# Loading the first tile of x in two column parts, and transposing the second tile among the first products

## The chip, the cores and the metric

The kernel runs on one core of one Trainium2 chip. The metric is the device time of one execution in microseconds (us). Three executions of the kernel before took 219.65, 219.71 and 219.72 us, median 219.71.

## What is computed

x is 2048 x 640, bf16. It is normalised by rows (LayerNorm without weights); on the result run a linear attention of 32 heads of 20 columns and a ReLU feed-forward of width 1728, and the two are joined:

```python
x = A_x
xn = _layernorm(x, axis=-1)
s = _A_ref(xn, A_wqkv, A_wo)              # q,k,v = xn @ wqkv; phi(q), phi(k); o = num / den; o @ wo
g = _silu(_B_ref(xn, B_w1, B_w2))         # relu(xn @ w1) @ w2
return x + s * g
```

What matters here is the beginning of the second branch, h = relu(xn @ w1), for the first 512 rows of x. A row's scale (one over its standard deviation) is positive and can be applied after the ReLU, so for these rows the kernel multiplies w1 with x minus its row mean, and applies the scale later (`rsy`).

## The kernel before

x is cut into 16 tiles of 128 rows (`t`), its 640 columns into 5 chunks of 128 (`C`). TensorE needs x transposed: `xnT` holds it as 5 chunks of 128 columns by 2048 rows. h is computed transposed, in 13 blocks `f` of 128 columns of w1 (and a half one) by 512 rows of x (`j`). All matmuls of one block add up over the 5 chunks in one of the 8 banks of PSUM (`ps[b]`).

The order of the work is written out by hand. `Sched` only collects, for each engine, its operations in the order of the calls, and derives the waits from the keys that each operation reads (`R`) and writes (`W`); each engine then runs its own list strictly in order. There are two queues that issue DMAs: SyncE's (SP), on which nearly all are issued, and ScalarE's (ACT).

The start, in the lines that the change touches:

- Loads (lines 370 to 375): x0 on SP, x1 on ACT, x2 on SP, the first piece of w1 (384 columns, blocks 0 to 2) on ACT, the second piece (256 columns, blocks 3 and 4) and x3 on SP. `x_load` is line 337, `w1_load` and `w_load` lines 364 and 341.
- `fill` (line 356) issues matmuls of constants, whose result nobody reads. Line 614 asks for nine.
- `T_mean` (line 422): the row mean of one tile, as a pass that scales by 1/640 and accumulates; on VectorE for tile 0 (line 428), on ScalarE for the others (line 424). `center` (line 434) subtracts the mean from some chunks, on VectorE (line 435). `T_pe` (line 439) transposes chunks on TensorE into a bank (line 441). `T_copy` (line 444) brings them from the bank to `xnT`, on ScalarE (line 448) or VectorE (line 451).
- `H_mm` (line 574) multiplies chunks `ks` of one block of w1 with columns of `xnT`; its matmuls are line 575. `H_first(t, fs, ks)` (line 608) does that for the 128 rows of tile t and the blocks fs; after tile 3 the block goes through ReLU on ScalarE (line 582).

The calls of lines 614 to 656 give the order: fillers; mean, centring, transposes and copies of tile 0, with those of tile 1 right behind; then the products of tile 0 with blocks 0 to 2; then tile 1's products, tile 2's transposes, and so on, with the later blocks and tiles behind. `w_load` of the key weights (line 628) waits for the second centring of tile 0, `w1_load(2)` (line 634) for the centring of tile 2, and the loads of x4 to x7, the last piece of w1 and the query weights are queued on SP behind them. `LN_stats` and `LN_norm` (lines 394 and 411) compute the exact mean and variance of a tile on VectorE later, and read the same tiles of x.

Of the kernel before, what the change touches and what calls it, by code (L numbers as in the profile page):

```python
# [210 lines left out]
def bass_recurrent_scan__linear_attn_block__dense_activation_relu__prompt_kernel(  # L211
# [14 lines left out]
    P = 128  # L226
# [75 lines left out]
    mhalf = nc.alloc_sbuf_tensor("mhalf", [P, 1], f32)  # L302
    denS = nc.alloc_sbuf_tensor("denS", [P, 512], f32)
    rden = nc.alloc_sbuf_tensor("rden", [P, 512], bf)
    mean = nc.alloc_sbuf_tensor("mean", [P, 4], f32)
    stats = nc.alloc_sbuf_tensor("stats", [P, T, 2, 6], f32)
    mv = nc.alloc_sbuf_tensor("mv", [P, T, 2], f32)
    rsv = nc.alloc_sbuf_tensor("rsv", [P, T], f32)
# [22 lines left out]
    def tok(t):  # L331
        return slice(P * t, P * (t + 1))
# [4 lines left out]
    def x_load(t, extra=(), E="SP"):  # L337
        sl = t % XR
        return dma(E, lambda eng: eng.dma_start(xin[:, sl, :], x2[tok(t), :]), W=[("xin", sl)], extra=extra)
# [16 lines left out]
    def fill(n, w=512):  # L356
        sc.group("PE", [(lambda eng: eng.matmul(ps[0][:, 0:w], lhsT=cones, rhs=cwide[:, 0:w], start=True, stop=True))
                        for _ in range(n)], W=[("ps", 0)])
# [5 lines left out]
    def w1_load(i, extra=(), E="SP"):  # L364
        w_load(w1_sb[:, :, W1C[i]:W1C[i + 1]], B_w1[:, W1C[i]:W1C[i + 1]], ("w1", i), extra, E)
# [1 line left out]
    def w1_part(f):  # L367
        return [i for i in range(NP) if W1C[i] <= P * f < W1C[i + 1]][0]

    x_load(0)  # L370
    x_load(1, E="ACT")
    x_load(2)
    w1_load(0, E="ACT")
    w1_load(1)
    x_load(3)

# [17 lines left out]
    def LN_stats(t):  # L394
        xv = xin[:, t % XR, :]
        for a in range(2):
            sc.op("DVE", lambda eng, a=a: eng.bn_stats(stats[:, t, a, :], xv[:, HN * a:HN * (a + 1)]),  # L397
                  R=[("xin", t % XR)], W=[("stats", t, a)])
        sc.op("DVE", lambda eng: eng.bn_aggr(mv[:, t, :], stats[:, t, :, :].rearrange("p a b -> p (a b)")),
              R=[("stats", t, 0), ("stats", t, 1)], W=[("mv", t)])  # L400
        sc.op("POOL", lambda eng: eng.tensor_scalar(out=rsv[:, t:t + 1], in0=mv[:, t, 1:2], scalar1=EPS_LN,
                                                    scalar2=None, op0=ALU.add), R=[("mv", t)], W=[("rsv", t)])
        sc.op("POOL", lambda eng: eng.tensor_tensor(out=rsy[:, t:t + 1], in0=rsv[:, t:t + 1], in1=mhalf[:, :],
                                                    op=ALU.pow), R=[("rsv", t), ("mhalf",)], W=[("rsy", t)])
# [3 lines left out]
    def xnk(t, cs=range(C)):  # L408
        return [("xn", t, c) for c in cs]

    def LN_norm(t, turn=False):
        last_norm[0] = sc.op("DVE", lambda eng: eng.tensor_scalar(
            out=xn[:, t, :], in0=xin[:, t % XR, :], scalar1=mv[:, t, 0:1], scalar2=rsy[:, t:t + 1],
            op0=ALU.subtract, op1=ALU.mult), R=[("xin", t % XR), ("mv", t), ("rsy", t)], W=xnk(t))
        if turn:
            xnT_dma(t)
        elif t + XR < T:
            x_load(t + XR)

    def T_mean(t, E="ACT"):
        if E == "ACT":
            sc.op("ACT", lambda eng: eng.activation(out=ek[:, 0, 0, :], in_=xin[:, t, :], func=ACTF.Copy, scale=1.0 / D,
                                                    accum_out=mean[:, t:t + 1]),
                  R=[("xin", t)], W=[("mean", t), ("ek_e", 0)])
        else:
            sc.op("DVE", lambda eng: eng.tensor_scalar(out=ek[:, 1, 0, :], in0=xin[:, t, :], scalar1=1.0 / D, scalar2=0.0,
                                                       op0=ALU.mult, op1=ALU.add, accum_out=mean[:, t:t + 1]),
                  R=[("xin", t)], W=[("mean", t), ("ek_e", 1)])  # L430

    sc.allow_unread.update([("ek_e", 0), ("ek_e", 1)])

    def center(t, c0, c1):
        return sc.op("DVE", lambda eng: eng.tensor_scalar(
            out=xn[:, t, P * c0:P * c1], in0=xin[:, t, P * c0:P * c1], scalar1=mean[:, t:t + 1], scalar2=None,
            op0=ALU.subtract), R=[("xin", t), ("mean", t)], W=xnk(t, range(c0, c1)))

    def T_pe(t, c0, c1, b):
        psb = ps[b].bitcast(bf)  # L440
# [3 lines left out]
    def T_copy(E, t, c0, c1, b):  # L444
        out = xnT[:, c0:c1, tok(t)]
        src = ps[b].bitcast(bf)[:, P * c0:P * c1].rearrange("p (c q) -> p c q", c=c1 - c0)
        if E == "ACT":
            sc.op("ACT", lambda eng: eng.activation(out=out, in_=src, func=ACTF.Copy), R=[("ps", b)],
                  W=xtk(t, range(c0, c1)))
        else:  # L450
            sc.op("DVE", lambda eng: eng.tensor_copy(out, src), R=[("ps", b)], W=xtk(t, range(c0, c1)))
# [159 lines left out]
            if t == 3:  # L611
                H_ev(0, f, HF[f])

    fill(9)
    T_mean(0, "DVE")
    T_mean(1)
    center(0, 0, 2)
    T_pe(0, 0, 2, 7)
    held = center(0, 2, 5)
    T_pe(0, 2, 5, 1)  # L620
    T_copy("ACT", 0, 0, 2, 7)
    center(1, 0, C)
    T_copy("DVE", 0, 2, 5, 1)
    T_pe(1, 0, 2, 0)
    T_pe(1, 2, 5, HF[4])
    T_copy("ACT", 1, 0, 2, 0)
    T_copy("DVE", 1, 2, 5, HF[4])
    w_load(wqk[:, :, D:2 * D], A_wqkv[:, D:2 * D], ("wk",), [held])
    H_first(0, (0, 1, 2), (0, 1))
    H_first(0, (0, 1, 2), (2, 3, 4))  # L630
    T_mean(2)
    held = center(2, 0, C)
    H_first(1, (0, 1, 2))
    w1_load(2, [held])
    x_load(4)
    x_load(5)
# [467 lines left out]
```

## Time and profile before

| what | value |
|---|---|
| median of three executions | 219.71 us |
| the profiled execution, its own time | 219.73 us |
| its span | 217.9 us |
| ScalarE's first pass over tile 2 (line 424) | starts at 6.18 us |
| ScalarE's copy of tile 3 (line 448) | starts at 9.76 us |
| key products (line 466) | start at 12.07 us |

The span runs from the first to the last instruction that the profiler recorded. In rows of the timeline the first number is the start and the second the duration in us; then come the engine, the line of the kernel, the operation, what it writes and reads, and in brackets how long the engine had been idle and what ended that. Here "psT" is PSUM, "reg" stands for several buffers (x, w1, xn, xnT), "SPq" and "ACTq" are the queues on which SyncE and ScalarE issue DMAs. PE is TensorE, PEld its weight loads, DVE VectorE, ACT ScalarE, POOL GpSimd.

### The profile page before, as it was taken

Reading aid. Unit: us, or ns where it says so; the run is one execution under the profiler, and the core shown is the slowest. Engines: PE = TensorE matmul, PEld = TensorE weight load, DVE = VectorE, ACT = ScalarE, POOL = GpSimd, SP = SyncE. Lnnn points to the kernel's source line nnn. Section 1 sums busy time; section 2 is a strip of 40 time slices with the busy share of each in tenths; the row PEclk is TensorE's granted clock in tenths of the full one; section 3 lists DMA queues with packets and bytes.
Section 4 is the critical chain, followed back from the end, with each engine's and each line's share of the span. In section 5 each row is a group of like instructions: output and inputs, shape, how many; then the busy total and the mean of one; then the engine's idle time right before and its main releaser. Section 6 shows DMA issues by size and latency. Waiting matters only on the chain.

```text
span 217.9 us, 3064 instructions
## 1 busy us (share of the span) xinstructions
PE 213.2 (98%) x1195; PEld 109.2 (50%) x1215; DVE 106.5 (49%) x196; ACT 92.8 (43%) x179; POOL 28.5 (13%) x59
## 2 busy tenths in 40 slices
PE   8999999999999999999999999999999999999995
PEld 2975444444444444444464446544444446555574
DVE  2788899994894757666700005711121122230354
ACT  3577558666775669955321213514110211101220
POOL 1155022041110000100000000000000003960001
DMA  6998668612236423660069988769312113334152
GB/s 204 292 386 130 150 178 206 138 24 51 54 79 120 84 51 78 120 140 0 3 194 365 232 146 256 288 188 352 52 24 44 31 24 65 69 115 148 24 168 91
DMA packets 48491, 29.24 MB, mean 134 GB/s; under 512 B 31492, under 2 KB 47836, under 8 KB 48476
## 3 DMA queue, kind: packets, MB, share of 16 engines
q1 hardware_dynamic: 47532, 28.29, 49.6%
q10 hardware_dynamic: 944, 0.75, 1.0%
q8 instruction: 9, 0.15, 0.3%
q14 instruction: 6, 0.05, 0.1%
HBM read 15.75 MB, written 5.24 MB: 96 GB/s over the span
## 4 chain that ended last, share of the span: by engine, by line
PE 96%; DMA 1%; DVE 1%; issue 1%
PE psT L575 26%; PE psT L879 19%; PE psT L560 10%; PE psT L829 8%; PE psT L503 7%; PE psT L922 7%; PE psT L886 7%; PE psT L957 3%; PE psT L466 2%; PE psT L818 2%; DMA reg<-in_A_x_dram 1%; PE psT L597 1%; PE psT L901 1%; PE psT L838 1%; PE psT L849 1%; PE psT L441 1%
## 5 line engine op out<-in xcount | busy, mean ns | idle before, releaser
L575 PE MATMUL psT<-reg 128*128 128x512 bf16 (+1 forms) x328 | 60.5, 330 | 0.5 <-issue 0.2
L879 PE MATMUL psT<-hT,reg 128*128 128x512 bf16 x191 | 44.2, 379 | 0.3
L575 PEld LDWEIGHTS psT<-reg 128*128 128x128 bf16 x335 | 28.6, 98 | 27.5 <-issue 0.4
L582 ACT ACTIVATE hT<-psT 128x512 bf16<-128x512 f32 x52 | 30.6, 598 | 16.0 <-PE psT L575 15.9
L929 DVE TENSOR_TENSOR er<-psT,ek 128x512 bf16<-128x512 f32 x15 | 10.4, 692 | 48.4 <-PE psT L922 45.2
L879 PEld LDWEIGHTS psT<-hT,reg 128*128 128x128 bf16 x195 | 18.9, 98 | 22.3 <-issue 0.7
L917 ACT ACTIVATE ek<-psT 128x512 bf16<-128x512 f32 x15 | 8.3, 599 | 42.3 <-PE psT L904 21.9
L560 PE MATMUL psT<-reg 128*128 128x512 bf16 x100 | 24.8, 379 | 0.0
L937 POOL TENSOR_TENSOR reg<-reg 128x640 bf16<-128x640 bf16 x8 | 10.9, 1392 | 90.9 <-DMA reg<-er 90.9
L568 DVE TENSOR_SCALAR er<-psT 128x512 bf16<-128x512 f32 x20 | 13.7, 686 | 8.9 <-ACT er L567 8.9
L503 PE MATMUL psT<-reg 128*128 128x512 bf16 x72 | 17.8, 379 | 0.2
L922 PE MATMUL psT<-pqT,reg 128*128 128x512 bf16 x71 | 17.3, 379 | 0.2
L829 PE MATMUL psT<-reg 128*128 128x512 bf16 x78 | 17.3, 379 | 0.1
L560 PEld LDWEIGHTS psT<-reg 128*128 128x128 bf16 x100 | 9.8, 98 | 11.8
L886 PE MATMUL psT<-reg,hT 128*128 128x320 bf16 x104 | 15.3, 299 | 0.0
L512 DVE TENSOR_SCALAR ek<-psT 128x512 bf16<-128x512 f32 x15 | 10.1, 676 | 9.3 <-ACT ek L511 9.3
L567 ACT ACTIVATE er<-psT 128x512 bf16<-128x512 f32 x20 | 12.0, 598 | 5.5 <-PE psT L560 5.5
L397 DVE BATCH_NORM_STATS2 stats<-reg 128x6 f32<-128x320 bf16 x32 | 13.8, 474 | 0.7 <-DMA reg<-in_A_x_dram 0.6
L570 DVE SCALAR_TENSOR_TENSOR pqT<-er 128x512 bf16<-128x512 bf16 x20 | 13.8, 692 | 0.7
L841 DVE TENSOR_TENSOR reg<-psT,m 120x120 bf16<-120x120 f32 x6 | 1.7, 282 | 23.4 <-PE psT L838 23.4
L886 PEld LDWEIGHTS psT<-reg,hT 128*128 128x128 bf16 x104 | 10.1, 98 | 4.8 <-issue 0.3
L829 PEld LDWEIGHTS psT<-reg 128*128 128x128 bf16 x80 | 7.8, 98 | 9.3
(77 smaller groups left out, 183.4 us busy)
## 6 DMA issues: line engine op xcount, KB each, us to landing
rscr<-rden SPq DMA_DIRECT2D x4, 640.0 KB, 8.2
reg<-rscr SPq DMA_DIRECT2D x5, 512.0 KB, 6.8
reg<-in_A_x_dram SPq DMA_DIRECT2D x4, 640.0 KB, 6.1
reg<-in_A_x_dram SPq DMA_DIRECT2D x15, 160.0 KB, 3.2
out_dram<-reg SPq DMA_DIRECT2D x15, 160.0 KB, 1.9
reg<-in_A_wqkv_dram SPq DMA_DIRECT2D x2, 800.0 KB, 4.7
reg<-in_B_w_dram SPq DMA_DIRECT2D x1, 1120.0 KB
reg<-in_B_w_dram SPq DMA_DIRECT2D x1, 960.0 KB, 8.0
```

What stands on the lines that cost most here:

```text
L397: sc.op("DVE", lambda eng, a=a: eng.bn_stats(stats[:, t, a, :], xv[:, HN * a:HN * (a + 1)]), R=[("xin", t % XR)], W=[("stats", t, a)])
L503: lastK[0] = sc.group("PE", [(lambda eng, k=k: eng.matmul(ps[b], lhsT=wqk[:, k, D + P * m:D + P * (m + 1)], rhs=xnT[:, k, schunk(j)], star ...
L560: sc.group("PE", [(lambda eng, k=k: eng.matmul(ps[b], lhsT=wqk[:, k, P * f:P * (f + 1)], rhs=rhs(k), start=(k == 0), stop=(k == C - 1))) f ...
L567: sc.op("ACT", lambda eng: eng.activation(out=e_, in_=ps[b], func=ACTF.Exp), R=[("ps", b)], W=[("er_e", es)])
L568: sc.op("DVE", lambda eng: eng.tensor_scalar(out=r_, in0=ps[b], scalar1=0.0, scalar2=1e-6, op0=ALU.max, op1=ALU.add), R=[("ps", b), ("er_e ...
L570: sc.op("DVE", lambda eng: eng.scalar_tensor_tensor(out=pqT[:, f, schunk(j)], in0=e_, scalar=1.0, in1=r_, op0=ALU.min, op1=ALU.add), R=[(" ...
L575: return sc.group("PE", [(lambda eng, k=k: eng.matmul(ps[b][:, lo:hi], lhsT=w1_sb[:, k, P * f:P * (f + 1)], rhs=xnT[:, k, 512 * j + lo:512 ...
L582: sc.op("ACT", lambda eng: eng.activation(out=hT[:, f, schunk(j)], in_=ps[b], func=ACTF.Relu), R=[("ps", b)], W=[("hT", j, f)])
L829: ag = sc.group("PE", [(lambda eng, t=t: eng.matmul(ps[b][:, 0:KW], lhsT=xn[:, t, P * k:P * (k + 1)], rhs=pk[:, t, 0:KW], start=(t == 0), ...
L879: sc.group("PE", [(lambda eng, f=f: eng.matmul(ps[b], lhsT=w2_sb[:, f, P * m:P * (m + 1)], rhs=hT[:, f, schunk(j)], start=(f == 0 and not ...
L886: sc.group("PE", [(lambda eng, f=f: eng.matmul(ps[b][:, 0:HN], lhsT=hT[:, f, tok(t)], rhs=w2_sb[:, f, HN * n:HN * (n + 1)], start=(f == 0 ...
L922: sc.group("PE", [(lambda eng, c=c: eng.matmul(ps[b], lhsT=wf[:, c, P * m:P * (m + 1)], rhs=pqT[:, c, schunk(j)], start=(c == 0), stop=(c ...
```

## The change

- Tile 0 of x is loaded by two DMAs: columns 0 to 383 on SP, columns 384 to 639 on ACT. x1 moves to SP behind the first part, ahead of x2; on ACT the first piece of w1 follows the second part. The order on SP is then x0 (part), x1, x2, second piece of w1, x3.
- The mean of tile 0 is summed in two: VectorE takes the first part (`T_mean0`), ScalarE the second (`T_mean(0)`), into two columns of `mean`; `center` of tile 0 subtracts both.
- Eight fillers in place of nine.
- Tile 0's first copy (two chunks) moves from ScalarE to VectorE, the second (three chunks) from VectorE to ScalarE. Tile 1's first copy moves from ScalarE to VectorE, so that VectorE does both.
- The transposes of tile 1 are issued between the products of tile 0 with chunks 0, 1 and those with chunks 2, 3, 4. The products of tile 1 with blocks 0 to 2 are split in the same way: chunks 0, 1 of all three blocks first.
- The load of the key weights is called before the transposes of tile 1.

```diff
-    mean = nc.alloc_sbuf_tensor("mean", [P, 4], f32)
+    mean = nc.alloc_sbuf_tensor("mean", [P, 5], f32)
...
-    x_load(0)
-    x_load(1, E="ACT")
+
+    X0 = ((0, 3 * P), (3 * P, D))
+    x0k = [("x0", 0), ("x0", 1)]
+
+    def x0_load(a, E):
+        lo, hi = X0[a]
+        dma(E, lambda eng: eng.dma_start(xin[:, 0, lo:hi], x2[tok(0), lo:hi]), W=[x0k[a]])
+
+    def xk(t):
+        return [("xin", t % XR)] + (x0k if t == 0 else [])
+
+    x0_load(0, "SP")
+    x0_load(1, "ACT")
+    x_load(1)
+    w1_load(0, E="ACT")
     x_load(2)
-    w1_load(0, E="ACT")
     w1_load(1)
     x_load(3)
...
+    def T_mean(t):
+        lo, hi = X0[1] if t == 0 else (0, D)
+        m = 4 if t == 0 else t
+        sc.op("ACT", lambda eng: eng.activation(out=ek[:, 0, 0, lo:hi], in_=xin[:, t, lo:hi], func=ACTF.Copy,
+                                                scale=1.0 / D, accum_out=mean[:, m:m + 1]),
+              R=[x0k[1] if t == 0 else ("xin", t)], W=[("mean", m), ("ek_e", 0)])
+
+    def T_mean0():
+        lo, hi = X0[0]
+        sc.op("DVE", lambda eng: eng.tensor_scalar(out=ek[:, 1, 0, lo:hi], in0=xin[:, 0, lo:hi], scalar1=1.0 / D,
+                                                   scalar2=0.0, op0=ALU.mult, op1=ALU.add, accum_out=mean[:, 0:1]),
+              R=[x0k[0]], W=[("mean", 0), ("ek_e", 1)])
...
     def center(t, c0, c1):
         return sc.op("DVE", lambda eng: eng.tensor_scalar(
-            out=xn[:, t, P * c0:P * c1], in0=xin[:, t, P * c0:P * c1], scalar1=mean[:, t:t + 1], scalar2=None,
-            op0=ALU.subtract), R=[("xin", t), ("mean", t)], W=xnk(t, range(c0, c1)))
+            out=xn[:, t, P * c0:P * c1], in0=xin[:, t, P * c0:P * c1], scalar1=mean[:, t:t + 1],
+            scalar2=mean[:, 4:5] if t == 0 else None, op0=ALU.subtract,
+            **(dict(op1=ALU.subtract) if t == 0 else {})),
+            R=xk(t) + [("mean", t)] + [("mean", 4)] * (t == 0), W=xnk(t, range(c0, c1)))
...
-    fill(9)
-    T_mean(0, "DVE")
+    fill(8)
+    T_mean0()
+    T_mean(0)
     T_mean(1)
     center(0, 0, 2)
     T_pe(0, 0, 2, 7)
     held = center(0, 2, 5)
     T_pe(0, 2, 5, 1)
-    T_copy("ACT", 0, 0, 2, 7)
+    T_copy("DVE", 0, 0, 2, 7)
+    T_copy("ACT", 0, 2, 5, 1)
     center(1, 0, C)
-    T_copy("DVE", 0, 2, 5, 1)
+    w_load(wqk[:, :, D:2 * D], A_wqkv[:, D:2 * D], ("wk",), [held])
+    H_first(0, (0, 1, 2), (0, 1))
     T_pe(1, 0, 2, 0)
     T_pe(1, 2, 5, HF[4])
-    T_copy("ACT", 1, 0, 2, 0)
-    T_copy("DVE", 1, 2, 5, HF[4])
-    w_load(wqk[:, :, D:2 * D], A_wqkv[:, D:2 * D], ("wk",), [held])
-    H_first(0, (0, 1, 2), (0, 1))
     H_first(0, (0, 1, 2), (2, 3, 4))
     T_mean(2)
+    T_copy("DVE", 1, 0, 2, 0)
+    T_copy("DVE", 1, 2, 5, HF[4])
     held = center(2, 0, C)
-    H_first(1, (0, 1, 2))
+    H_first(1, (0, 1, 2), (0, 1))
+    H_first(1, (0, 1, 2), (2, 3, 4))
     w1_load(2, [held])
```

More of the change, by code (lines that the diff above doesn't have):

```diff
@@ L397, in LN_stats @@
             sc.op("DVE", lambda eng, a=a: eng.bn_stats(stats[:, t, a, :], xv[:, HN * a:HN * (a + 1)]),
-                  R=[("xin", t % XR)], W=[("stats", t, a)])
+                  R=xk(t), W=[("stats", t, a)])
         sc.op("DVE", lambda eng: eng.bn_aggr(mv[:, t, :], stats[:, t, :, :].rearrange("p a b -> p (a b)")),
@@ L413, in LN_norm @@
             out=xn[:, t, :], in0=xin[:, t % XR, :], scalar1=mv[:, t, 0:1], scalar2=rsy[:, t:t + 1],
-            op0=ALU.subtract, op1=ALU.mult), R=[("xin", t % XR), ("mv", t), ("rsy", t)], W=xnk(t))
+            op0=ALU.subtract, op1=ALU.mult), R=xk(t) + [("mv", t), ("rsy", t)], W=xnk(t))
         if turn:
@@ L418, in LN_norm @@
             x_load(t + XR)
[L422 to L430, printed above, removed]
+    def T_mean(t):
[9 more added lines that the diff above has]
+              R=[x0k[0]], W=[("mean", 0), ("ek_e", 1)])
     sc.allow_unread.update([("ek_e", 0), ("ek_e", 1)])
```

## The prediction

> **What bounds the kernel now.** I read the page first, then TensorE's waits, then the chain from the last instruction back, and last the first 12 us instruction by instruction. The page:
>
> ```profile
> span 217.9 us, 3064 instructions
> PE 213.2 (98%) x1195; PEld 109.2 (50%) x1215; DVE 106.5 (49%) x196; ACT 92.8 (43%) x179; POOL 28.5 (13%) x59
> PE 96%; DMA 1%; DVE 1%; issue 1%
> ```
>
> TensorE is busy 213.2 of 217.9 us, and 96% of the chain is its own work. Its waits over the whole span:
>
> ```profile
> PE psT L357 <- PEq L1089: 0.8, 1, 0.8
> PE psT L441 <- DVE reg L435: 0.2, 1, 0.2
> PE psT L575 <- issue: 0.2, 1, 0.2
> ```
>
> So it waits only at the start: 0.8 us before the first filler, and 0.2 us before the first transposes. Everything after about 5.3 us is one unbroken run of matmuls. The end of the kernel is therefore the moment at which that run gets going, plus a fixed amount of work. The chain of that start:
>
> ```profile
> 0.79 3.03 DMA reg<-in_A_x_dram
> 3.84 0.84 DVE ek L428 x2
> 4.71 0.30 DVE reg L435
> 5.05 0.98 PE psT L441 x10
> 6.03 1.74 PE psT L575 x30
> 7.77 0.28 PE psT L441 x5
> ```
>
> Tile 0 of x lands at 3.82 (0.79 + 3.03), VectorE sums it until 4.67, centres it, and TensorE transposes it. The change works on exactly these rows. The timeline of the stage, each row an instruction or a run of them (start, duration):
>
> ```profile
> 3.84 0.82 DVE L428 TENSOR_SCALAR_CACHE_REDUCE ek<-reg 128x640 bf16<-128x640 bf16 x1 [3.84 <-DMA reg<-in_A_x_dram]
> 4.03 0.74 ACT L424 ACTIVATE ek<-reg 128x640 bf16<-128x640 bf16 x1 [1.02 <-DMA reg<-in_A_x_dram]
> 4.67 0.19 ACT L424 ACTIVATION_READ_ACCUMULATOR ek<-reg 128x1 f32 x1
> 4.71 0.29 DVE L435 TENSOR_SCALAR reg<-reg,mean 128x256 bf16<-128x256 bf16 x1
> 5.05 0.68 PE L441 MATMUL psT<-ident,reg 128*128 128x128 bf16 x5 [0.23 <-DVE reg L435]
> 5.48 0.38 ACT L448 ACTIVATE reg<-psT 128x256 bf16<-128x256 bf16 x1 [0.62 <-PE psT L441]
> 5.77 0.36 DVE L451 COPY reg<-psT 128x384 bf16<-128x384 bf16 x1 [0.25 <-PE psT L441]
> 5.92 1.85 PE L575 MATMUL psT<-reg 128*128 128x128 bf16 x30
> 7.03 0.39 DVE L435 TENSOR_SCALAR reg<-reg,mean 128x640 bf16<-128x640 bf16 x1 [0.61 <-ACT ek L424]
> 7.61 0.44 PE L441 MATMUL psT<-ident,reg 128*128 128x128 bf16 x5
> ```
>
> The reader should see two marks. The first product (L575) starts at 5.92, right behind ScalarE's copy (5.48 + 0.38 = 5.86), after ten transposes, five of tile 0 and five of tile 1. The transposes of tile 2 start at 7.61, after 30 products without a gap: (1.85 - 0.22) / 29 = 0.056 us each, where 0.22 is the length of a single one (below). I count the gain at this second mark, because the work before it is the same set in both kernels.
>
> TensorE's rate is not constant in this stage. First row: the fillers; then the transposes that start from 5.0 to 5.5, and those that run on behind 5.7 (durations min/median/max in ns):
>
> ```profile
> 0.83 4.00 PE L357 MATMUL psT<-const-bfloat16-1.0 128*128 128x512 bf16 x9 [0.83 <-PEq L1089]
> L441 PE MATMUL psT<-ident,reg x5: 268/289/314, 5.0 to 5.5; 128*128 128x128 bf16 x5
> L441 PE MATMUL psT<-ident,reg x6: 219/219/268, 5.5 to 5.8; 128*128 128x128 bf16 x6
> ```
>
> Nine fillers of 512 columns in 4.00 us are about 0.42 us apart, which for 128 columns is 0.107; the products run at 0.056. The transposes shorten from 314 to 219 ns within 5.0 to 5.8. So TensorE runs at half rate until about 5.6, and whatever is started before that is paid double.
>
> **The DMAs, and who gets there first.** Issues (the first four rows) and what two later ones took to land; then packets by queue between 3.4 and 4.9 us, q10 being ScalarE's queue and q1 SyncE's:
>
> ```profile
> 0.79 0.40 ACTq L339 DMA_DIRECT2D reg<-in_A_x_dram  x1
> 0.79 0.88 SPq L339 DMA_DIRECT2D reg<-in_A_x_dram  x2
> 1.22 0.47 ACTq L342 DMA_DIRECT2D reg<-in_B_w_dram  x1
> 1.71 0.43 SPq L342 DMA_DIRECT2D reg<-in_B_w_dram  x1
> reg<-in_B_w_dram ACTq DMA_DIRECT2D x1, 480.0 KB, 4.5
> reg<-in_A_x_dram SPq DMA_DIRECT2D x1, 160.0 KB, 3.2
> DMA packets 676, 0.55 MB, mean 369 GB/s; under 512 B 22, under 2 KB 676, under 8 KB 676
> q10 hardware_dynamic: 563, 0.43, 84.5%
> q1 hardware_dynamic: 113, 0.12, 22.4%
> ```
>
> The first piece of w1 (480 KB, ScalarE's queue) is issued at 1.22 and lands 4.5 later, at 5.72: only 0.2 ahead of the product that reads it. So the weights would be late next, as soon as the transposes come earlier. Tile 2 of x (SyncE's second, issued about 1.25) lands at about 4.45. SyncE's next one (L342, 1.71) was issued by 2.14, and yet between 3.4 and 4.9 five packets in six belong to w1 on ScalarE's queue. The transfers are served nearly one after another in the order of issue, at 369 GB/s.
>
> **The change, part by part.**
>
> *Tile 0 in two parts.* The two tiles x0 and x1 (320 KB) stood ahead of the first landing; now the two parts of x0 (160 KB) do. 160 KB at 369 GB/s are 0.44 us, so the landing gains between 0 and 0.44; I take 0.3, since the queues barely move in their first half microsecond. That gives 3.5 for SyncE's 384 columns; ScalarE's 256 have landed at 3.7 (x1 on that queue was 0.2 behind x0).
>
> *Its mean.* ScalarE's sum took 0.83 with its read (4.03 to 4.86) for 640 columns. For 256 it lies between 0.33 (in proportion) and 0.83; I take 0.45 with a fixed share. It ends at 4.19. VectorE's 384 columns take between 0.50 and 0.83 from 3.5, I take 0.56, and end at 4.07. ScalarE is last. The centring starts 0.04 later (the hand-over was 0.04 before), at 4.23 against 4.71: **0.48 earlier**. It now subtracts two scalars. No row shows that form; the same operation with two scalars in L412 takes 441 ns at 640 columns against 388 here, so at most 0.05 is added, and nothing taken.
>
> *Fillers.* One less: eight end at about 4.2. With nine the last would have run to 4.6, about where the transposes now start, so this removes a collision and costs nothing by itself.
>
> *Tile 0's transposes* start 0.05 behind the first centring (as before: 5.00 to 5.05), at 4.6, at half rate. *The copy* of its first two chunks moves from ScalarE to VectorE: it starts at 5.03 (0.43 behind the first transpose, as 5.05 to 5.48 before) and takes between 0.29 (256 columns in L435) and 0.36 (384 columns in L451); I take 0.30. Products could start at 5.39.
>
> *The weights.* ScalarE's queue has 96 KB less ahead of w1. Tile 2 of x is now the third of SyncE's and issued behind w1, where it was second and went ahead of it. By the service in order seen above w1 loses those 160 KB, 0.44 us, and lands at 5.28. No row shows what a product waits behind a landing; between the hand-overs above (0.05) and twice that, I take 0.1. Products start at 5.40. The two conditions meet, so from here further speed on either side gains nothing.
>
> *Tile 1's transposes among the products.* Before, the five ran in the time that TensorE waited for the first copy; now they run between products, in the unbroken run. So 35 matmuls stand between the first product and tile 2's transposes where 30 did: 35 x 0.056 = 1.96. And what runs from 5.40 to 5.60 is at half rate, which loses 0.10. Tile 2's transposes start at 5.40 + 1.96 + 0.10 = 7.46, against 7.61: **0.15 gained**.
>
> *What could be late inside that run.* x1 stands second on SyncE's queue and lands between 4.0 and 4.45; its mean on ScalarE (0.83) ends between 5.04 and 5.30, and queued behind it is the copy of tile 0's last three chunks (0.39), done by 5.76, due at 6.1. VectorE centres tile 1 behind its copy, 5.33 to 5.72; the transposes are due at 5.84. Tile 1's two copies, now both on VectorE, end at 6.45 and 6.8, due at 6.6 and 6.95. The centring of tile 2 follows on VectorE by 7.2, due at 7.46. Every margin is 0.1 to 0.3, so they hold, but none would survive a further 0.3. SyncE's wk load is released by the centring of tile 0, now about 0.45 earlier, and the second w1 piece behind tile 2's centring about 0.1 earlier; the loads behind them move along and so do not fall behind TensorE. Tile 3's transfer has the same bytes ahead of it as before.
>
> *Sum.* The profiled execution took 219.73 us (span 217.9 and 1.8 around it); less 0.15 it is 219.58. The median of the runs shown is 219.71, so I put 219.57 for a median.
>
> [...]
>
> **Rivals.**
>
> 1. *The parts come no earlier, or the queues share* (0.20). Then x1 and x2 still run beside w1, and it lands between 5.57 (only the 96 KB are saved, at half the share) and 5.72; or both halves of x0 land at the old 3.8 and 4.0 and the copy is ready at 5.65. Products start at 5.65 to 5.8 at full rate; 1.96 later is 7.61 to 7.76. Time 219.73 to 219.88: the five transposes in the run eat what is left. Against it: the row of 563 packets.
>
> 2. *The full rate comes late* (0.17): the slower side. TensorE reached full rate 4.8 us after its first filler (0.83 to 5.6), having stood still for about 0.4 us in all. Now it would stand from 4.2 to 4.6 and from about 5.1 to 5.4, 0.7 us. If the hardware asks for an activity that this falls short of, and counts anew from 5.4, the products run at half rate for another 4.8 us, losing 2.4 in place of 0.1: 219.58 + 2.3 = 221.9. It decides at one point: whether the 0.7 us are too much. For it: one filler less. Against it: the present pause did no harm. [...]
>
> 3. *The whole 0.48 arrives* (0.13): parts and weights land so early that products start by 5.17, and the full rate is there: 5.17 + 1.96 = 7.13, time 219.25. For it: every event ahead of the products does move that far. Against it: w1 would have to land by 5.07.
>
> **How the numbers follow.** Forecast 0.50, at 219.57, itself from 219.4 to 219.7 (copy or weights 0.1 to 0.2 off either way). Within 0.2% (0.44 us, about what a measurement of this kernel can tell from no change) lie the forecast and the first rival: 0.70. Faster by more: the third, 0.13. Slower by more: the second, 0.17. The range 219.2 to 220.0 takes in the first and third rivals and a lost margin of some tenths, and leaves out only the second.
>
> **What would show it.** In the new profile: the centring at about 4.2; the last release of the first product by w1 or by VectorE's copy at about 5.4; tile 2's transposes at about 7.46; products 0.056 apart from 5.6 on; no wait of TensorE behind that. I am wrong if products are still 0.107 apart at 7 us, if w1 lands behind 5.5, or if a stall stands between the products of tiles 0 and 1.

## The result, and the profile after

The changed kernel is slower: 22 executions have a median of 221.19 us, 22 of the kernel before beside them 219.75; the ratio is 1.0053, 95% interval 1.0032 to 1.0074. The ratios here and below leave out executions more than 1.5% above the fastest of their kernel: the one of 1290 us here, which is left out of everything else too, and one or two late ones each in e2, e8, e12, e14 and e18. Without the 1290 us the median is 220.68. A median hides what happened, though. The executions fall into two groups with a gap between them:

| | executions | below 221.2 us | above |
|---|---|---|---|
| before | 22 | 21: 219.40 to 221.03 | 1: 222.23 |
| changed | 21 | 11: 219.66 to 220.68 | 10: 221.69 to 222.77 |

I call the upper group late. The profiled execution, 219.80 us, is one of the lower group, and shows that group's side only. Lines of its page, and TensorE's waits:

```profile
span 218.0 us, 3087 instructions
...
PE 214.0 (98%) x1214; PEld 109.0 (50%) x1214; DVE 106.6 (49%) x197; ACT 93.0 (43%) x180; POOL 28.5 (13%) x59
...
PE 96%; DMA 1%; DVE 1%; ACT 0%; SPq 0%; issue 0%; ACTq 0%
```

```profile
PE psT L357 <- PEq L1108: 0.8, 1, 0.8
PE psT L592 <- DVE reg L450: 0.7, 1, 0.7
```

Again TensorE waits only at the start, but its wait of 0.2 us in front of the transposes has become one of 0.7 us in front of the first products (L592 here, L575 before). The timeline of the start (start, duration, both in us; in brackets the idle time before and what ended it):

```profile
3.15 0.55 DVE L443 TENSOR_SCALAR_CACHE_REDUCE ek<-reg 128x384 bf16<-128x384 bf16 x1 [3.15 <-DMA reg<-in_A_x_dram]
3.34 0.42 ACT L437 ACTIVATE ek<-reg 128x256 bf16<-128x256 bf16 x1 [0.33 <-DMA reg<-in_A_x_dram]
...
3.88 0.64 DVE L450 TENSOR_SCALAR reg<-reg,mean 128x256 bf16<-128x256 bf16 x2 [0.17 <-ACT ek L437]
...
4.29 0.79 PE L458 MATMUL psT<-ident,reg 128*128 128x128 bf16 x5
4.38 0.74 ACT L437 ACTIVATE ek<-reg 128x640 bf16<-128x640 bf16 x1 [0.54 <-DMA reg<-in_A_x_dram]
...
4.72 0.29 DVE L468 COPY reg<-psT 128x256 bf16<-128x256 bf16 x1 [0.20 <-PE psT L458]
...
5.74 0.50 PE L592 MATMUL psT<-reg 128*128 128x128 bf16 x6 [0.66 <-DVE reg L450]
...
6.07 0.44 PE L458 MATMUL psT<-ident,reg 128*128 128x128 bf16 x5
...
6.35 1.50 PE L592 MATMUL psT<-reg 128*128 128x128 bf16 x24
...
7.69 0.44 PE L458 MATMUL psT<-ident,reg 128*128 128x128 bf16 x5
```

Tile 0 is summed, centred and transposed 0.7 to 0.8 us earlier than before (centring 3.88 against 4.71). The first copy is done at 5.01. Still the products start at 5.74, only 0.18 earlier, and tile 2's transposes at 7.69 against 7.61. The profile puts the wait down to VectorE (L450, the centring of tile 1), but these products don't read that; the copy that they read was done at 5.01. Of what they need, w1 came last, issued at 1.23 and landed 4.4 later, at about 5.6:

```profile
reg<-in_B_w_dram ACTq DMA_DIRECT2D x1, 480.0 KB, 4.4
```

Why so late is in the DMA columns (last two: share and GB/s) of the stretches of 0.8 us from 2.6 on, first before, then after:

```profile
2.60:3.40 0.80, 0.80 (x4) 0.25 (x3) 0.00 (x0) 0.41 (x1) 0.00 (x0) 1.00 1.00 359
3.40:4.20 0.80, 0.80 (x4) 0.24 (x2) 0.36 (x1) 0.17 (x1) 0.00 (x0) 1.00 1.07 374
```

```profile
2.60:3.40 0.80, 0.80 (x4) 0.25 (x3) 0.25 (x1) 0.47 (x2) 0.00 (x0) 1.00 0.88 244
3.40:4.20 0.80, 0.80 (x3) 0.09 (x1) 0.63 (x4) 0.45 (x2) 0.00 (x0) 1.00 0.80 229
```

With less ahead of w1 the DMA engines deliver it hardly sooner (4.4 us after its issue, against 4.5); they move 229 to 244 GB/s where they moved 359 to 374. They are busy for less of the time (0.88 and 0.80 against 1.00 and 1.07), and for the same busy time they also move about a fifth less (244 / 0.88 = 277 against 359, 229 / 0.80 = 286 against 374 / 1.07 = 350). From 3.4 to 4.2 the packets of ScalarE's queue, 0.18 MB in both kernels, took longer: 229 of them had 77.3% of the 16 engines' time, 43 ns each, where 231 had 65.0%, 36 ns each, before.

### The profile page after: what moved, and what is told of

It is laid out like the page before. It is cut to its first block, busy times and chain, and to the rows that moved or that the text cites. A ratio compares the mean times of both kernels' runs of the same rounds, so it can differ in the third digit from the quotient of the medians.

```text
span 218.0 us, 3087 instructions
## 1 busy us (share of the span) xinstructions
PE 214.0 (98%) x1214; PEld 109.0 (50%) x1214; DVE 106.6 (49%) x197; ACT 93.0 (43%) x180; POOL 28.5 (13%) x59
## 4 chain that ended last, share of the span: by engine, by line
PE 96%; DMA 1%; DVE 1%; ACT 0%; SPq 0%; issue 0%; ACTq 0%
PE psT L592 26%; PE psT L898 19%; PE psT L577 10%; PE psT L848 8%; PE psT L520 7%; PE psT L941 7%; PE psT L905 7%; PE psT L976 3%; PE psT L483 2%; PE psT L837 2%; DMA reg<-in_A_x_dram 1%; PE psT L614 1%; PE psT L920 1%; PE psT L857 1%; PE psT L868 1%; PE psT L691 1%
## 5 line engine op out<-in xcount | busy, mean ns | idle before, releaser
L592 PE MATMUL psT<-reg 128*128 128x512 bf16 (+1 forms) x335 | 62.0, 331 | 0.7 <-DVE reg L450 0.7
L592 PEld LDWEIGHTS psT<-reg 128*128 128x128 bf16 x335 | 28.7, 98 | 28.3 <-DVE reg L450 0.9
L577 PE MATMUL psT<-reg 128*128 128x512 bf16 x100 | 24.8, 379 | 0.0
L520 PE MATMUL psT<-reg 128*128 128x512 bf16 x75 | 18.5, 379 | 0.0
L941 PE MATMUL psT<-pqT,reg 128*128 128x512 bf16 x75 | 18.1, 379 | 0.0
L848 PE MATMUL psT<-reg 128*128 128x512 bf16 x80 | 17.4, 379 | 0.0
```

Of the source, the lines that this page charges most:

```text
L520: lastK[0] = sc.group("PE", [(lambda eng, k=k: eng.matmul(ps[b], lhsT=wqk[:, k, D + P * m:D + P * (m + 1)], rhs=xnT[:, k, schunk(j)], star ...
L577: sc.group("PE", [(lambda eng, k=k: eng.matmul(ps[b], lhsT=wqk[:, k, P * f:P * (f + 1)], rhs=rhs(k), start=(k == 0), stop=(k == C - 1))) f ...
L592: return sc.group("PE", [(lambda eng, k=k: eng.matmul(ps[b][:, lo:hi], lhsT=w1_sb[:, k, P * f:P * (f + 1)], rhs=xnT[:, k, 512 * j + lo:512 ...
L848: ag = sc.group("PE", [(lambda eng, t=t: eng.matmul(ps[b][:, 0:KW], lhsT=xn[:, t, P * k:P * (k + 1)], rhs=pk[:, t, 0:KW], start=(t == 0), ...
L941: sc.group("PE", [(lambda eng, c=c: eng.matmul(ps[b], lhsT=wf[:, c, P * m:P * (m + 1)], rhs=pqT[:, c, schunk(j)], start=(c == 0), stop=(c ...
```

## The experiments

Theory A: in a late execution TensorE works at half rate far into the products (0.107 us for one of 128 columns in place of 0.056), because it stood still too long before them. Rival B: a transfer or wait of the new order comes late in some executions, and the rate has nothing to do with it. The kernel before ran beside every batch: of its 144 executions, the first 22 included, 2 were above 221.2.

**Fill the pause, or fill more ahead of it** (changed kernel):

```diff
     T_pe(0, 2, 5, 1)
+    fill(2)
```

> The changed kernel with two more fillers between tile 0's transposes and the first products, so that TensorE is busy in the pause of about 1 us that the new profile shows there (4.75 to 5.74). Theory A (the executions near 222 us are those in which the full rate of TensorE comes late, because the pause makes it stand still too long): the group near 222 us is gone or down to the before kernel's 1 or 2 in 10, and all executions lie between 219.4 and 220.7 us, median about 219.8. Rival B (the late group comes from a transfer or a wait of the new order, such as tile 1 or the first piece of w1 landing late in some executions): filling the pause changes nothing, about half of the executions stay near 222 us.

Measured: median 220.69, ratio 1.0018 (0.999 to 1.0046); 2 of 12 late (221.31, 222.62), the rest 219.58 to 220.95. Against 6 of 12 in the unchanged kernel beside it (below) the group thins out, as theory A says; but four of the rest lie above 220.7, the most that it allowed.

```diff
-    fill(8)
+    fill(9)
```

> The changed kernel with nine fillers in place of eight. Theory A: the pauses of TensorE before 5.7 us shrink by about 0.4 us (the first transposes start at about 4.6 in place of 4.3), so the share of executions near 222 us falls, to between none and a third; the others stay at 219.7 to 220.5 us since the first products wait for w1 at about 5.6 either way. Rival B: about half near 222 us, as with eight.

Measured: median 220.24, ratio 1.0007 (0.9991 to 1.0024); 1 of 12 late (223.04), the rest 219.69 to 220.71. As theory A has it, but for three of the rest, up to 0.2 us above its 220.5. Samples of 12 are small: by itself neither of the two shows the thinning, together they are 3 late of 24 against 24 of 59 in all samples of the unchanged kernel.

**Eight fillers in the kernel before**, nothing else:

> The kernel before with eight fillers in place of nine and nothing else changed: the one pause of TensorE, before the first transposes, grows from 0.43 to 0.86 us. Theory A: a group near 221.5 to 222 us appears, in a fifth to a half of the executions, beside 219.7 us. Rival B: as the kernel before, 219.7 us and at most 1 in 10 late.

Measured: median 220.1, ratio 1.0009 (0.9991 to 1.0028), 1 of 12 late (221.62). The profile (219.66 us) has a standstill of 0.62 us, its idle time ahead of the transposes, and the products run at full rate; here theory A expected more late executions.

**The changed kernel again**:

> The changed kernel once more, unchanged, for a second sample and for a profile of a late execution if one is caught. Both theories: two groups, near 220 and near 222 us, about half each. In a profile of a late execution theory A expects products of 128 columns 0.107 us apart until 8 to 10 us (0.056 in the profile at hand) with every transfer landing as before; rival B expects the products at 0.056 and a wait of about 2 us somewhere.

Measured: median 221.16, ratio 1.0054 (1.003 to 1.0079); six at 220.02 to 220.61 and six at 221.72 to 222.14. Its profile (220.04) is not a late one.

**Six fillers**, first in the changed kernel, then in the one before:

```diff
-    fill(8)    # the kernel before: fill(9)
+    fill(6)
```

> The changed kernel with six fillers in place of eight, so that TensorE stands still from 3.3 to 4.3 us as well as from 4.9 to 5.7; the fillers' results are read by nobody and no product moves. The profiles so far show the full rate arriving at another moment in each execution (4.6, 4.75, 5.1, 5.6 us). Theory A, now sharper (the full rate is granted at the end of a busy stretch whose start is not tied to the kernel; too much standstill in a stretch makes the next one count): nearly all executions are late, spread over 220.7 to 222.5 us, at most 2 in 12 below 220.4; a profile shows products 0.107 apart until between 7.7 and 11 us. Rival B (the late group has nothing to do with TensorE's activity): half near 220.0, half near 222, as with eight.

Measured: 6 of 6 late, 221.24 to 223.91, ratio 1.0117 (1.008 to 1.0155). In the profile (221.35) the products run at half rate until about 8.8 us (12 matmuls from 7 to 8, 14 from 8 to 9, 22 from 9 to 10). That the rate is granted at the end of a busy stretch was a guess of mine; no trace shows such a stretch.

> The kernel before with six fillers in place of nine: one pause of 1.7 us (3.3 to 5.0) before the first transposes, nothing else moved. Theory A: most executions late, 220.6 to 222.4 us, at most 3 in 12 below 220.4. Rival B: as the kernel before, 219.5 to 220.6.

Measured: median 221.07, ratio 1.0053 (1.003 to 1.0075); 9 of 12 between 220.89 and 221.98, 3 at 219.5 to 219.7. Taking three useless matmuls away from the kernel before, without moving any transfer, slows most of its executions by over 1 us, where none of 29 of the kernel before beside it is above 220.78. (Only five of the nine pass the mark of 221.2; I count all nine as late here.) Its profile is of one of the nine, 221.03 us:

```profile
0.82 2.72 PE L357 MATMUL psT<-const-bfloat16-1.0 128*128 128x512 bf16 x6 [0.82 <-PEq L1089]
4.87 1.27 PE L441 MATMUL psT<-ident,reg 128*128 128x128 bf16 x10 [1.33 <-DVE reg L435]
5.93 3.18 PE L575 MATMUL psT<-reg 128*128 128x128 bf16 x30
8.95 0.44 PE L441 MATMUL psT<-ident,reg 128*128 128x128 bf16 x5
```

Products start at 5.93, as in the kernel before (5.92), and the same 30 take 3.18 us in place of 1.85. That is theory A in one row, and rival B falls as a full explanation. (Six fillers also leave TensorE still for 1.33 us, the idle time in the row of the transposes, in place of 0.23.)

**Less w1 ahead of the first products**:

```diff
-    w1_load(0, E="ACT")
+    for h, (k0, k1) in enumerate(((0, 2), (2, C))):
+        dma("ACT", lambda eng, k0=k0, k1=k1: eng.dma_start(
...
+            W=[("w1", 0, h)])
...
```

The products then wait only for the part that they read.

> The changed kernel with the first piece of w1 loaded as two DMAs on ScalarE's queue, chunks 0 and 1 ahead of chunks 2 to 4, so that the first six products need only 192 of its 480 KB. It tests the second term: in the new profiles the products wait for w1 until 5.6 to 5.9 us. Theory A and the late w1: the first products start at 5.0 to 5.3 in place of 5.7 to 6.0, TensorE's pause shrinks to some 0.3 us, so the group near 222 us is gone, and the others are 0.05 to 0.2 us below the changed kernel's: median 219.6 to 219.9. If the copies and not w1 held the products: start unchanged at 5.7 to 6.0 and two groups as before.

Measured: median 220.42, ratio 1.0041 (1.0018 to 1.0063); 2 of 12 late. The first six products start at 5.27, so w1 did hold them; but the second part of w1, 288 KB, lands 5.2 us after its issue, the other products wait for it, and the pause has only moved behind the first ones. The median of 219.6 to 219.9 that I expected was missed:

```profile
5.27 0.82 PE L600 MATMUL psT<-reg 128*128 128x128 bf16 x6
5.88 0.60 PE L461 MATMUL psT<-ident,reg 128*128 128x128 bf16 x5
7.08 1.50 PE L600 MATMUL psT<-reg 128*128 128x128 bf16 x24 [0.59 <-DMA reg<-in_B_w_dram]
```

**The order of the transposes undone**:

```diff
-    H_first(0, (0, 1, 2), (0, 1))
     T_pe(1, 0, 2, 0)
     T_pe(1, 2, 5, HF[4])
+    H_first(0, (0, 1, 2), (0, 1))
     H_first(0, (0, 1, 2), (2, 3, 4))
```

> The changed kernel with tile 1's transposes ahead of the first products again, as in the kernel before: this undoes the change of order alone. The new profile has tile 1 centred at 5.64 and w1 landed at 5.6, so the transposes run at 5.7 to 6.0 and products start at 6.0 in place of 5.74: the 35 matmuls end at the same time. Theory A: two groups as in the changed kernel, the faster at 219.7 to 220.6 (within 0.1 of it), about half near 222 us, since the pause stays. If the order is what made the change slower: no late group, median near 219.9.

> The changed kernel with tile 1's transposes ahead of the first products, a second sample (the first had 1 late execution in 12, against the half that I expected). If the transposes, which need no w1, shorten the pause before w1 lands enough: again at most 2 in 12 late, median below the changed kernel's on the same chip by over 0.3 us. If the first sample was luck: about half late.

Measured: first 1 of 12 late (median 219.95, ratio 1.0007, 0.9995 to 1.0019), then 6 of 12 (median 221.18, ratio 1.0037, 1.0001 to 1.0073), where the unchanged kernel beside it had 4 of 12. The first sample was luck, and with samples of 12 a difference between 1 and 4 says little. The second profile is a late execution of another kind (222.36 us):

```profile
0.83 3.20 PE L357 MATMUL psT<-const-bfloat16-1.0 128*128 128x512 bf16 x8 [0.83 <-PEq L1108]
4.35 0.63 PE L458 MATMUL psT<-ident,reg 128*128 128x128 bf16 x5 [0.33 <-DVE reg L450]
6.68 0.53 PE L458 MATMUL psT<-ident,reg 128*128 128x128 bf16 x5 [1.70 <-DVE reg L450]
7.00 3.41 PE L592 MATMUL psT<-reg 128*128 128x128 bf16 x30
10.21 0.51 PE L458 MATMUL psT<-ident,reg 128*128 128x128 bf16 x5
10.55 1.56 PE L592 MATMUL psT<-reg 128*128 128x128 bf16 x25
```

```profile
L357 PE MATMUL psT<-const-bfloat16-1.0 x8: 381/634/634, 0.8 to 3.6; 128*128 128x512 bf16 x8
```

```profile
6.00:7.00 1.00, 0.32 (x5) 0.32 (x6) 0.39 (x1) 1.00 (x4) 0.00 (x0) 0.96 1.12 368
7.00:8.00 1.00, 1.00 (x13) 1.00 (x11) 0.90 (x3) 0.51 (x3) 0.00 (x0) 0.50 1.07 383
8.00:9.00 1.00, 1.00 (x12) 1.00 (x11) 0.00 (x0) 0.61 (x2) 0.00 (x0) 0.50 1.05 358
9.00:10.00 1.00, 1.00 (x13) 1.00 (x11) 0.00 (x0) 0.00 (x0) 0.00 (x0) 0.50 0.89 156
10.00:11.00 1.00, 1.00 (x18) 1.00 (x16) 0.25 (x1) 0.00 (x0) 0.00 (x0) 0.83 1.00 336
```

The second fence is the row of the fillers (shortest, median and longest in ns), the third the stretches of 1 us, with the granted clock (the share of TensorE's full rate that the hardware allowed) third from the right. The full rate is there by 3.6 (the last filler takes 381 ns, not 634), then after tile 0's transposes, TensorE stands still for 1.7 us, and the granted clock goes from 1.00 to 0.50 for 3.4 us: 0.08 + 3.00 + 0.34, since a mean of 0.96 over 1 us is 0.08 us at half. All 30 products run at half rate. Here the full rate was there and was lost again.

This gives a mark for both kinds. In these profiles the column shows a rate that is taken away (0.50 above), not one that has not come yet: it is 1.00 in the late profile of six fillers above, whose full rate had not come yet (12 products in 1 us), as it is under the first fillers of the kernel before and of the changed one (1.00 from 0.83 to 2.19, at 634 ns a filler). The stretch in the profile of six fillers:

```profile
7.00:8.00 1.00, 1.00 (x12) 1.00 (x11) 0.38 (x1) 0.83 (x2) 0.00 (x0) 1.00 0.95 321
```

Over a whole execution 3.4 us at half are 0.8%, a mean of 0.992. Of the 24 late executions of the unchanged kernel in all samples 19 have 1.000 and 5 have 0.992. So five lost the full rate again. In the other 19 it will have come late; the mark can't tell that from a mere wait, and only one of the 19 has a profile (e15 below, where it is so).

**The order alone, and the parts alone.** The kernel before with only the new order of transposes, products and copies:

> The kernel before with the change of order alone: tile 1's transposes among the products and the copies moved between VectorE and ScalarE, with the old loads, the old mean and nine fillers. Products start at 5.8 to 5.9 as before, but with the five transposes inside the run, so tile 2's transposes start 0.2 to 0.3 later (7.8 to 7.9). Theory A: no pause beyond 0.5 us, so at most 1 in 12 late, and the rest 0.2 to 0.3 us above the kernel before (median 219.9 to 220.1). If the order by itself made the group near 222 us: a third to a half of the executions there.

Measured: none of 12 late, 219.84 to 220.22, median 219.96 against 219.78 beside it, ratio 1.0005 (0.9995 to 1.0016); tile 2's transposes start at 7.88. The order costs its five transposes and makes no late group.

The parts with other loads, tile 1's transposes ahead of the first products and nine fillers, as before (the lines show the loads only):

```diff
-    x_load(1)
-    w1_load(0, E="ACT")
+    x_load(1, E="ACT")
     x_load(2)
+    w1_load(0, E="ACT")
```

> A version made to beat both: tile 0 in two parts, but tile 1 on ScalarE's queue again and tile 2 second on SyncE's, tile 1's transposes ahead of the first products, and nine fillers, so that TensorE has something to do from 4.6 to 5.8 but for some 0.5 us. Theory A with w1 as the bound: the first products start when w1 has landed, 5.7 to 6.0 us, no five transposes inside the run; at most 1 in 12 late, the rest 219.5 to 220.3, median within 0.2 of the kernel before and not clearly below it. If the early centring were worth its 0.48: median near 219.3.

Measured: a miss, 6 of 6 between 222.65 and 225.39, ratio 1.0177 (1.0145 to 1.0209). As ScalarE's third DMA, w1 was issued 0.5 us later and landed 6.9 after that, although from 6 to 9 us the DMA engines moved 366 to 396 GB/s. The products waited until 8.61 (2.46 us of standstill) and then ran at half rate.

> The changed kernel a third time, beside the next run on the same chip. Theory A: a third to two thirds of the executions between 221.5 and 222.8 us, the rest 219.7 to 220.7.

The last is the unchanged kernel beside them. Measured: 4 of 12 late (221.72 to 222.38), median 220.29, ratio 1.0046 (1.0018 to 1.0073).

**Which transfer?** In the late profile above tile 1 had landed late, at about 5.3. I formed theory C, a race between tile 1 and w1: where w1 is served first, tile 1 is late, and that alone makes the standstill. Two orders of issue on SyncE's queue test it:

```diff
     x_load(1)
-    w1_load(0, E="ACT")
+    w1_load(0)
     x_load(2)
```

(and, in the second kernel, `w1_load(0)` ahead of `x_load(1)`)

> The changed kernel with the first piece of w1 on SyncE's queue behind tile 1 of x (in place of ScalarE's queue), so that tile 1 is always served first. Theory C (the late group is made by a race: tile 1 and w1 are issued at the same moment on two queues, and where w1 goes first, tile 1 lands 1 us later, TensorE stands still till 6.7 and loses the full rate): the late group is gone, at most 1 in 12 above 221; tile 1 is summed from 3.9 to 4.5; median 219.8 to 220.3. Theory A alone (the pause while w1 is awaited is enough): the pause stays, so a third or more are late.

Measured: 5 of 5 late, 221.94 to 223.03, ratio 1.0117 (1.0101 to 1.0133), although tile 1 was summed from 3.84; w1, now issued 0.5 us later (1.72), landed at about 6.1, and products started at 6.27, after 1.23 us of standstill, at half rate. Theory C has fallen.

> The changed kernel with the first piece of w1 on SyncE's queue ahead of tile 1, so that tile 1 always loses. Theory C: nearly all executions late, 221.5 to 222.8 us; in the profile tile 1 is summed from about 5.3, tile 1's transposes start at 6.5 to 6.8, and products run at 0.107 for 3 us or so. Theory A alone: as the changed kernel, about half late.

Measured: 7 executions, 3 at 220.87 to 220.89 and 4 at 222.38 to 224.48, ratio 1.0072 (1.0046 to 1.0099). Here tile 1 is the late one (summed from 5.69), and that does it as well, though in 4 of 7 and not in nearly all. Either transfer can make the standstill. The profile (222.38) is again of the second kind: the first six products still run at full rate, then the granted clock is 0.50 from 7.28 to 10.68, 3.4 us once more (its means are 0.64 from 7 to 8, 0.50 from 8 to 10 and 0.66 from 10 to 11):

```profile
5.29 0.50 PE L592 MATMUL psT<-reg 128*128 128x128 bf16 x6 [0.46 <-DMA reg<-in_B_w_dram]
7.00 0.50 PE L458 MATMUL psT<-ident,reg 128*128 128x128 bf16 x5 [1.22 <-DVE reg L450]
7.29 2.77 PE L592 MATMUL psT<-reg 128*128 128x128 bf16 x24
```

e9 is of the same kind, at half from 8.28 to 11.7 (means of 0.64 from 8 to 9, 0.50 from 9 to 11 and 0.83 from 11 to 13).

**Two more profiles of the changed kernel**:

> The changed kernel unchanged, one look. If it is a late execution (221.5 us or more): theory C expects ScalarE's pass over tile 1 to start at 5.2 us or later and half rate in the products; theory A alone expects that pass at 3.9 to 4.7 and half rate; rival B a wait of about 2 us at full rate. If it is not late, the pass starts at 3.9 to 4.7 by all of them.

> The changed kernel unchanged, a further look, with the same expectations as the look before it.

The first caught a late execution of the changed kernel itself, 222.20 us; the second was 219.98. The late one, TensorE's part of the timeline:

```profile
4.29 0.79 PE L458 MATMUL psT<-ident,reg 128*128 128x128 bf16 x5
6.67 0.80 PE L592 MATMUL psT<-reg 128*128 128x128 bf16 x6 [1.59 <-DMA reg<-in_B_w_dram]
7.26 0.74 PE L458 MATMUL psT<-ident,reg 128*128 128x128 bf16 x5
7.79 2.48 PE L592 MATMUL psT<-reg 128*128 128x128 bf16 x24
10.11 0.44 PE L458 MATMUL psT<-ident,reg 128*128 128x128 bf16 x5
```

Its DMA issues and its stretch of 3.4 to 4.2 us:

```profile
reg<-in_B_w_dram ACTq DMA_DIRECT2D x1, 480.0 KB, 5.3
```

```profile
3.40:4.20 0.80, 0.80 (x3) 0.09 (x1) 0.65 (x4) 0.69 (x3) 0.00 (x0) 1.00 0.79 189
```

Tile 1 is early (summed from 3.96). w1 takes 5.3 us to land, 0.9 more than in the other profile; from 3.4 to 4.2 the DMA engines move 189 GB/s. Tile 2's transposes start at 10.11 against 7.69: 2.42 later, and the execution is 2.40 longer. Its mean granted clock is 1.000, the first kind. Of the 2.42, 0.93 is the later start (6.67 against 5.74), and 1.49 the half rate (3.44 against 1.95 from there to 10.11).

**Is it the late w1 or the pause?** Theory D was that w1 lands late only where its first packets meet idle DMA engines. Tile 2's 160 KB were put back ahead of it, by loading tiles 1 and 2 with one DMA:

```diff
-    x_load(1)
+    dma("SP", lambda eng: eng.dma_start(xin[:, 1:3, :], x2[P:3 * P, :].rearrange("(t p) n -> p t n", p=P)),
+        W=[("xin", 1), ("xin", 2)])
     w1_load(0, E="ACT")
-    x_load(2)
```

> The changed kernel with tiles 1 and 2 loaded by one DMA on SyncE's queue, so that tile 2's 160 KB go ahead of w1 as in the kernel before; tile 1 is then known to have landed only with tile 2, at about 4.4. Theory D (the late group needs a w1 that lands late, and w1 lands late and unsteadily where its first packets meet idle DMA engines; behind a steady stream it lands 4.4 to 4.5 after its issue): products start at 5.7 to 5.9, at most 2 in 12 late, the rest within 0.5 us of each other at 219.8 to 220.3. If the pause of about 0.9 us is enough by itself: a third or more late, as in the changed kernel beside it. If the order of the bytes has nothing to do with it: w1 lands 4.2 to 5.3 after its issue as before and the share of late executions is unchanged.

> The changed kernel unchanged, as the control on the same chip. All theories: a third to two thirds of the executions at 221.5 to 222.8 us, the rest 219.7 to 220.7; in its profile the start of the products follows w1's landing by about 0.1 us.

Measured: 5 of 5 late, 221.77 to 222.78, ratio 1.0122 (1.0105 to 1.0138), and 3 of 12 in the unchanged kernel beside it (median 220.53, ratio 1.004, 1.0015 to 1.0065). The profile, 221.77 us:

```profile
4.27 0.79 PE L458 MATMUL psT<-ident,reg 128*128 128x128 bf16 x5
6.08 0.80 PE L592 MATMUL psT<-reg 128*128 128x128 bf16 x6 [1.02 <-DVE reg L450]
7.21 2.62 PE L592 MATMUL psT<-reg 128*128 128x128 bf16 x24
9.66 0.44 PE L458 MATMUL psT<-ident,reg 128*128 128x128 bf16 x5
```

w1 landed 4.7 after its issue, no later than in profiles of the lower group, and the products start at 6.08. Theory D has fallen too. w1 needn't be very late: here a standstill of 1.02 us in front of the products did it, where the full rate had not come yet (transposes of 0.79 us). Its price is the same sum as above: 9.66 - 7.69 = 1.97, and 221.77 - 219.80 = 1.97.

## Why the prediction was wrong

*What bounds it, and where to count.* Right. (The third row of waits before, 0.2 us at L575, lies behind 100 us and not at the start, which changes nothing.) In 19 of the 20 profiles the time less the start of tile 2's transposes is 212.07 to 212.15 us; the other is e14 (212.53), where the half rate goes on behind that mark. In the profile of the lower group 35 matmuls behind the first product take 1.95 (forecast 1.96).

*Tile 0 in two parts and its mean.* Right in kind, too small: centring at 3.88, 0.83 earlier, not 0.48. The parts landed 2.3 and 2.5 us after their issue; I had kept most of the first 3.0. The sizes of the two sums were right or nearly so (they ended at 3.7 and 3.85, 0.56 and 0.51 long; forecast 0.56 and 0.45). The forecast's own addition has a slip here, 3.7 and 0.45 give 4.15 and not 4.19, which changes nothing, since w1 set the start. A sum of the first rival has a small slip as well: saving half of 0.27 us lets w1 land at 5.59 and not 5.57.

*The weights.* **The first step that failed**: "By the service in order seen above w1 loses those 160 KB, 0.44 us, and lands at 5.28." It landed at 5.6 in the first profile, 4.4 after its issue in place of about 4.05, and 4.2 to 5.3 after its issue in the other five. (A landing behind 5.5 was one of the signs of being wrong that I had named.) I read the order of service as a queue whose length sets the landing. It held for who goes first (554 of the 575 packets from 3.4 to 4.9 were ScalarE's in the first profile), not for when: with less ahead, the DMA engines ran at 189 to 292 GB/s from 2.6 to 4.2 in five profiles (first, e4, e11, e15, e16), where they had run at 359 and 374. So products began at 5.74, and the five transposes inside the run cost more than was gained: the lower group is at 219.80 in the profile, where I had 219.58. Why the DMA engines were slower there is open.

*The full rate.* **The step that decided**: I gave "The full rate comes late" 0.17, with a standstill of 0.7 us in all, and left only this rival out of the range. Both of its ends moved against it. The transposes came earlier than forecast and the products later, so the standstill between them was 0.5 to 1.6 us by itself. The products did run at half rate, as in this rival, but that the price agrees (221.9 forecast, 221.69 to 222.77 in the first sample) is in part luck: I had put 2.3 us down to the half rate alone, where in e15 it has 1.49 and the later w1 0.93. A count of activity that starts anew and takes another 4.8 us is shown by no run: by an estimate from the matmuls in each us (12 at half rate, 22 at full, 14 or 17 where it changes) the half rate ended 2.8 to 3.4 us behind the first product in e5, e6, e15 and e17. What I had wrong is that it needn't decide one way: over all samples of the unchanged kernel 24 of 59 executions are late. And the 0.7 us that I had added up held only if both ends came as forecast; nothing in the forecast allowed for a pause that grows when one of them moves.

*Other waits.* Right in the six profiles of this kernel: behind the first products TensorE waits for no transfer and no other engine, in either group.

The runs show that the half rate carries more than half of the loss in the late profile of the changed kernel (1.49 of 2.42 us) and nearly all of it in e6 (products start at 5.93 against 5.92), and that standstill makes it frequent: none of 12 late with the order alone (0.1 us of wait), 1 of 12 with 0.6 (e3), about 2 in 5 with 0.5 to 1.6 in the changed kernel, 9 of 12 with 1.3 (e6), 4 of 7 with 0.5 and 1.2 (e14), and every execution of the two kernels whose profiles have 1.0 and 1.2 us (e13, e17), of the one with 2.5 (e9) and of the one with two pauses of 0.7 and 0.9 (e5). They don't show the rule by which the rate is granted. Three profiles of the lower group (e4, e11, e18) stood still for 1.1 to 1.3 us and kept the full rate, all of them with that rate there before the pause, as the length of the transposes tells (0.63 in place of 0.79):

```profile
4.15 0.63 PE L458 MATMUL psT<-ident,reg 128*128 128x128 bf16 x5
6.07 0.49 PE L592 MATMUL psT<-reg 128*128 128x128 bf16 x6 [1.30 <-DMA reg<-in_B_w_dram]
```

Those that had not got it before a pause of 1.0 or more went on at half (e6, e13, e15, e17), and in e9, e12 and e14 it was there and was lost. The idle times in the rows of these profiles, added up from the first filler on, sort them: 1.7 us or more where the rate was lost (0.46 and 1.22 in e14, 0.33 and 1.70 in e12, 0.51 and 2.46 in e9), up to 1.3 where it was there and was kept (e18), 1.0 to 1.6 where it had not come yet and the products went on at half (1.02 in e17, 1.59 in e15, 0.70 and 0.92 in e5), and up to 0.7 where it came with the products or ahead of them (0.66 in the first profile, 0.62 in e3). That is an order of the profiles at hand; no run tests it.

No version beat the kernel before; e2, nine fillers, comes nearest to it among those with tile 0 in parts (1.0007, 0.9991 to 1.0024), but for the first sample of e8, which did not repeat.

## What to carry to other kernels

Work that is brought forward on TensorE's path opens a pause behind it if what is next can't follow, and the pause can cost more than the step was worth (here centring came 0.83 us earlier, the standstill in front of the products was 0.5 to 1.6 us, and in e15 the half rate behind it cost 1.49): in a stage where the full rate still comes or goes, add up the standstill that a change leaves, not only the wait that it removes. A transfer need not come sooner when less is queued ahead of it: without tile 2's 160 KB ahead, w1 took 4.2 to 5.3 us to land, where it had taken 4.5. And where a kernel has two groups of executions, one profile shows one of them: read the list of times first, and get a profile of each.

## What was not expected of the hardware

The moment at which TensorE gets its full rate isn't tied to the kernel: by the lengths of its matmuls it came by 3.6 us (e12), at about 4.5 (e4), between 4.8 and 5.7 (after) and at 5.6 (before), and between 8.7 and 9.9 in the late profiles that had not got it before (e5, e6, e13, e15, e17); e4, the first profile and e15 are the same kernel. In e9, e12 and e14 the granted clock went to half for 3.4 us and was back at 10.3 to 11.7, behind pauses of 2.46 us (e9), of 1.70 (e12) and of 0.46 and 1.22 (e14); e4, e11 and e18 kept the rate through pauses of 1.10 to 1.30.

The DMA engines were busy and yet slow: from 3.4 to 4.2 us a share of 0.79 moved 189 GB/s in the late execution (e15), one of 1.07 moved 374 in the kernel before, which is 239 against 350 for a full share. The same 480 KB landed between 4.2 and 5.3 us after issue in the changed kernel, where the kernel before and the three others with its loads have 4.4 or 4.5.
